# Turning TensorE's branch round so that the usual path follows in place

## The chip, the cores and the metric

The kernel runs on one core of one Trainium2 chip. The metric is the device time of one execution in microseconds, of several executions; "fast" runs are those that the record marks as such, as it does every run in this study (the granted clocks that it lists are 0.996 to 1.000). A ratio is the mean time of one kernel's fast runs over that of the other kernel's fast runs of the same rounds, so it is not quite the ratio of the medians that are quoted beside it. The interval behind a ratio is the 95% interval.

## The reference, cut to what matters

A transformer block with modulation: attention over a window of cached keys and values, then a feed-forward part with ReLU.

```python
mod = (silu(c) @ w_mod).reshape(1, 6, 1, -1)        # sa, ca, ga, sb, cb, gb
h = layernorm(x) * (1 + ca) + sa
x = x + ga * A(h, k_cache, v_cache, wq, wo)         # 32 query heads, 8 kv heads, window 512
h = layernorm(x) * (1 + cb) + sb
x = x + gb * (relu(h @ w1) @ w2)                    # 2048 rows, 512 -> 1792 -> 512
```

## The kernel before

The kernel has a fast path, which leaves the maximum out of the softmax, and a general path, which is right for any input. A flag computed on the chip tells whether the fast path's values were in range. Every engine loads the flag at a "cut" in its instruction stream, and branches. With these inputs the flag is 128 and the fast path's last part is all that is left to run.

```python
def engine(name, e):
    stream, n_ops = fast[name], cut[name]
    kb.emit(stream, e, 0, n_ops)                 # up to the cut
    e.wait_ge(sems[flag_ev[0]], flag_ev[1])
    v = e.value_load(flag[0:1, 0:1])             # L1829
    with e.If(v != 128):                         # L1830: not taken with these inputs
        kb.emit(stream, e, n_ops)
        ...                                      # all engines meet
        gkb.emit(general[name], e)               # the general path
    with e.Else():
        kb.emit(stream, e, n_ops)                # the usual path: a jump away
```

In the built program TensorE's stream has 3946 instructions up to the branch, 2997 in the first arm (last part and general path) and 225 in the second. TensorE's cut lies in the feed-forward part, in front of an output group:

```python
def y_group(b, tl, c0=0, c1=D, deng=None):       # 14 matmuls, then two VectorE operations
    for fc in range(FC):
        mm(bank[bk][:, c0:c1], h1T[...], w2_sb[:, fc, c0:c1], ...)
    kb.op(DVE, ... yt = bank * gbf ...)          # L1723, "evacuation"
    kb.op(DVE, ... yo = yt + x ...)              # L1725
    dma(ov[:, t, c0:c1], yo, ..., eng=deng)      # output, from SyncE's or ScalarE's queue

# the last group is split, so that the kernel's last matmuls are short
for a in ((0, D // 2, ACT), (D // 2, 3 * D // 4, SP), (3 * D // 4, D, ACT)): ...
```

At the end SyncE waits until the outputs have landed; then all engines meet (each with a DRAIN; TensorE's takes 1.2 us, from 555.55 to 556.74, and so ends 0.05 us after its last matmul, whose modelled end is at 556.69) and the program ends.

## Time and profile before

| | before |
|---|---|
| time, median | 560.52 us (3 runs, known when the prediction was made), 560.68 us (5 runs, those of the result) |
| span in the profile | 559.4 us |
| TensorE's branch, as recorded | 3.44 us |
| gap that it leaves between matmuls | 0.19 us |
| TensorE done / SyncE last at the end | 556.7 / 559.1 us |

TensorE's sequencer, which hands instructions to its array, is some way ahead of it: it loads the flag at 510.1 us, and the last matmul in front of the branch starts at 513.74, 3.6 us later. This lead is called run-ahead below.

### The profile page before, as it was taken

Reading aid. Unit: us, or ns where it says so; the run is one execution under the profiler, and the core shown is the slowest. Engines: PE = TensorE matmul, PEld = TensorE weight load, DVE = VectorE, ACT = ScalarE, POOL = GpSimd, SP = SyncE. Lnnn points to the kernel's source line nnn. Section 1 sums busy time; section 2 is a strip of 40 time slices with the busy share of each in tenths; the row PEclk is TensorE's granted clock in tenths of the full one; section 3 lists DMA queues with packets and bytes.
Section 4 is the critical chain, followed back from the end, with each engine's and each line's share of the span. In section 5 each row is a group of like instructions: output and inputs, shape, how many; then the busy total and the mean of one; then the engine's idle time right before and its main releaser. Section 6 shows DMA issues by size and latency. Waiting matters only on the chain.

```text
span 559.4 us, 9666 instructions
## 1 busy us (share of the span) xinstructions
PE 550.5 (98%) x4060; PEld 315.8 (56%) x4134; DVE 253.8 (45%) x551; ACT 348.9 (62%) x453; POOL 54.7 (10%) x53
## 2 busy tenths in 40 slices
PE   8999999999999999999999999999999999999998
PEld 4665555555555555555555555555555654444444
DVE  4455555553546544335445443333354448321134
ACT  4986666666666666666666666666666644432500
POOL 3000022004410000033000000332000000000000
DMA  9897763513114144352352412111215110210001
GB/s 268 248 207 174 143 169 46 114 39 76 40 38 76 39 73 117 58 133 57 94 95 57 76 40 39 39 39 38 39 39 76 39 30 0 44 34 23 22 29 47
DMA packets 113309, 42.67 MB, mean 76 GB/s; under 512 B 93928, under 2 KB 112104, under 8 KB 113256
## 3 DMA queue, kind: packets, MB, share of 16 engines
q1 hardware_dynamic: 112024, 40.82, 34.3%
q10 hardware_dynamic: 1232, 1.15, 0.6%
q8 instruction: 33, 0.54, 0.4%
q14 instruction: 20, 0.16, 0.1%
HBM read 18.35 MB, written 2.10 MB: 37 GB/s over the span
## 4 chain that ended last, share of the span: by engine, by line
PE 98%; issue 1%; DMA 1%; DVE 0%; SPq 0%; DVEq 0%
PE psS L1372 28%; PE psO L1372 27%; PE psQ L1372 23%; PE psW L1372 20%; DMA c_row<-in_c_dram 1%; DVE qT L1611 0%; DVE hT L1630 0%; SPq L1303 0%; DVE PT L1723 0%; DVE PT L1725 0%; PE psS L1375 0%; PE psO L1416 0%; DVE modc L1438 0%; DVEq L123 0%
## 5 line engine op out<-in xcount | busy, mean ns | idle before, releaser
L1493 ACT ACTIVATE PT<-psS 128x1024 bf16<-128x1024 f32 x256 | 262.7, 1028 | 128.2 <-PE psS L1372 128.1
L1372 PE MATMUL psS<-qT,kT 128*128 128x512 bf16 x508 | 150.9, 379 | 0.5 <-DVE qT L1611 0.4
L1372 PEld LDWEIGHTS psO<-v,PT 128*128 128x128 bf16 x2048 | 126.6, 98 | 30.2
L1372 PE MATMUL psO<-v,PT 128*128 128x129 bf16 x2048 | 137.0, 220 | 0.0
L1372 PE MATMUL psQ<-hT,wq 128*128 128x512 bf16 (+1 forms) x510 | 130.5, 377 | 0.3 <-DVE hT L1630 0.2
L1503 DVE RECIPROCAL rinv<-psO 128x4 f32<-128x4 f32 x128 | 23.3, 182 | 227.2 <-PE psO L1372 227.2
L1372 PE MATMUL psW<-wo,oT 128*128 128x512 bf16 x454 | 118.1, 379 | 3.0
L1504 DVE TENSOR_TENSOR o<-psO,rinv 128x512 bf16<-128x512 f32 x128 | 88.5, 691 | 4.9 <-DVE rinv L1503 0.5
L1372 PEld LDWEIGHTS psQ<-hT,wq 128*128 128x128 bf16 x512 | 49.9, 98 | 60.3 <-issue 0.6
L1372 PEld LDWEIGHTS psS<-qT,kT 128*128 128x128 bf16 x512 | 49.5, 98 | 58.9 <-ACT PT L1493 0.7
L1485 ACT ACTIVATE qT<-psQ 128x512 bf16<-128x512 f32 x126 | 74.7, 593 | 0.0
L1712 ACT ACTIVATE wq<-psS 128x512 bf16<-128x512 f32 x56 | 33.4, 597 | 49.3 <-PE psS L1372 48.9
L1372 PEld LDWEIGHTS psW<-wo,oT 128*128 128x128 bf16 x512 | 45.0, 98 | 32.9 <-DVE acc L1526 1.2
L1526 DVE TENSOR_TENSOR acc<-psW,acc 128x512 f32<-128x512 f32 x48 | 33.2, 691 | 6.5 <-PE psW L1372 6.5
L1372 PE MATMUL psO<-wmw,wq 128*128 128x512 bf16 (+1 forms) x165 | 32.8, 352 | 0.3
L1529 POOL TENSOR_TENSOR acc<-acc,gaf 128x512 f32<-128x512 f32 x12 | 15.6, 1303 | 146.7 <-DVE acc L1526 139.8
L1388 POOL TENSOR_TENSOR rstd<-rstd,cst 128x4 f32<-128x4 f32 x7 | 7.2, 1025 | 216.8 <-DVE rstd L1387 216.8
L1723 DVE TENSOR_TENSOR PT<-psO,gbf 128x512 f32<-128x512 f32 (+1 forms) x12 | 7.5, 624 | 40.4 <-PE psO L1372 40.4
L1372 PE MATMUL psS<-h2T,wmw 128*128 128x512 bf16 x109 | 25.0, 379 | 0.2
L1372 PEld LDWEIGHTS psO<-wmw,wq 128*128 128x128 bf16 x168 | 15.3, 98 | 16.5
L1372 PE MATMUL psS<-hT,wmw 128*128 128x512 bf16 x110 | 24.4, 379 | 0.1
L1382 DVE BATCH_NORM_STATS2 st<-x 128x6 f32<-128x512 bf16 x31 | 21.1, 681 | 4.8 <-DMA x<-in_A_x_dram 4.8
(85 smaller groups left out, 192.6 us busy)
## 6 DMA issues: line engine op xcount, KB each, us to landing
wo<-in_A_wo_dram SPq DMA_DIRECT2D x4, 1024.0 KB, 5.9
wq<-in_A_wq_dram SPq DMA_DIRECT2D x7, 512.0 KB, 4.6
wmw<-in_B_w_dram SPq DMA_DIRECT2D x14, 256.0 KB, 3.1
wmw<-in_w_mod_dram SPq DMA_DIRECT2D x5, 512.0 KB, 4.8
oT<-o SPq DMA_TRANSPOSE x128, 2.4
out_dram<-PT SPq DMA_DIRECT2D x15, 128.0 KB, 1.7
x<-in_A_x_dram SPq DMA_DIRECT2D x3, 512.0 KB, 4.3
v<-in_A_v_cache_dram SPq DMA_DIRECT2D x8, 128.0 KB, 3.8
```

Of the source, the lines that this page charges most:

```text
L1372: kb.op(PE, lambda e: e.matmul(out_ap, lhsT, rhs, start=start, stop=stop), reads=reads, group_writes=[R_b[k] for k in bk], signal=signal)
L1382: kb.op(DVE, lambda e: e.bn_stats(st[:, t, :], x_sb[:, t, :]), reads=[R_x[t]], writes=[R_st[t]])
L1388: kb.op(POOL, lambda e: e.tensor_tensor(rstd[:, sl], rstd[:, sl], cst[:, 0:1].to_broadcast([P, hi - lo]), op=ALU.pow), reads=R_rstd[sl] + ...
L1485: kb.op(ACT, lambda e: e.activation(qT[u % NQT][:, :], bank[bk], ACTF.Copy), reads=[R_b[bk]], writes=[R_qT[u % NQT]])
L1493: kb.op(ACT, lambda e: e.activation(PT[u % NPT][:, pr * 2:pr * 2 + 2, :], s_ps[pr][:, :, :], ACTF.Exp, scale=scale), reads=[R_b[pr * 2], R ...
L1503: kb.op(DVE, lambda e: e.reciprocal(rinv[:, u, :], o_ps[:, :, P]), reads=[R_b[5], R_b[6]], writes=[R_rinv])
L1504: kb.op(DVE, lambda e: e.tensor_tensor(o_sb[u % NOS][:, :, :], o_ps[:, :, 0:P], rinv[:, u, :].unsqueeze(2).to_broadcast([P, TPB, P]), op=A ...
L1526: kb.op(DVE, lambda e: e.tensor_tensor(acc[:, tl, :], bank[WBK], acc[:, tl, :], op=ALU.add), reads=[R_b[WBK], R_acc[tl]], writes=[R_acc[tl]])
L1529: kb.op(eng, lambda e: e.tensor_tensor(acc[:, tl, :], acc[:, tl, :], gaf[:, :], op=ALU.mult), reads=[R_acc[tl], R_ga], writes=[R_acc[tl]])
L1712: kb.op(ACT, lambda e: e.activation(h1T[b % 2][:, fc, :], bank[bk], ACTF.Relu), reads=[R_b[bk]], writes=[R_h1[b % 2][fc]], pre=all_events( ...
L1723: kb.op(DVE, lambda e: e.tensor_tensor(yt[i][:, c0:c1], bank[bk][:, c0:c1], gbf[:, c0:c1], op=ALU.mult), reads=[R_b[bk], R_gb], writes=[R_ ...
```

## The change

The intent is to take the jump of 3.44 us, and the fetch of its target (one packet on TensorE's instruction queue in 510.6 to 514.1 us), out of TensorE's usual path. The usual path follows the branch in place; the general path lies behind it and is jumped over at the end.

```diff
-                with e.If(v != 128):
+                def last_part():
+                    kb.emit(stream, e, n_ops)
+                def rerun():
                     kb.emit(stream, e, n_ops)
...
                     gkb.emit(general[name], e)
-                with e.Else():
-                    kb.emit(stream, e, n_ops)
+                if name == "pe":
+                    with e.If(v == 128):
+                        last_part()
+                    with e.Else():
+                        rerun()
+                else:
+                    with e.If(v != 128):
+                        rerun()
+                    with e.Else():
+                        last_part()
```

## The prediction

> **What bounds the kernel now.** I read the page first: busy times and the chain that ended last.

> ```profile
> PE 550.5 (98%) x4060; PEld 315.8 (56%) x4134; DVE 253.8 (45%) x551; ACT 348.9 (62%) x453; POOL 54.7 (10%) x53
> PE 98%; issue 1%; DMA 1%; DVE 0%; SPq 0%; DVEq 0%
> ```

> TensorE is the bound: its matmuls are 98% of the span and 98% of the chain. A change to TensorE's branch can matter only by gaps that the branch leaves between matmuls, or by what follows the last matmul. So next I read the source-line views of the flag's load, of the branch and of the block's end, which also list what is not counted as busy.

> The flag's load on TensorE (kind and count; least, median and largest ns; first and last start in us):

> ```profile
> L1829 PEldq TENSOR_LOAD <-flag x1: 493/493/493, 510.1 to 510.1; - x1
> ```

> The branch on the five engines:

> ```profile
> L1830 POOLq COMPARE_BRANCH  x1: 53/53/53, 478.9 to 478.9; - x1
> L1830 ACTq COMPARE_BRANCH  x1: 50/50/50, 508.9 to 508.9; - x1
> L1830 PEldq COMPARE_BRANCH  x1: 3440/3440/3440, 510.6 to 510.6; - x1
> L1830 DVEq COMPARE_BRANCH  x1: 72/72/72, 521.7 to 521.7; - x1
> L1830 SPq COMPARE_BRANCH  x1: 53/53/53, 522.8 to 522.8; - x1
> ```

> TensorE's branch is on record with 3440 ns, the others' with 50 to 72 ns. The reader should see the tempting number here: 3.44 us in a branch on the engine that is the bound. But what counts is when matmuls run. The timeline of 513.6 to 514.3 us:

> ```profile
> 513.31 0.81 PE L1372 MATMUL psO<-wmw,wq 128*128 128x512 bf16 x3
> 513.52 0.10 PEld L1372 LDWEIGHTS psO<-wmw,wq 128*128 128x128 bf16 x1
> 514.14 0.11 PEld L1372 LDWEIGHTS psQ<-wmw,wq 128*128 128x128 bf16 x2 [0.52 <-issue]
> 514.15 0.39 PE L1372 MATMUL psQ<-wmw,wq 128*128 128x512 bf16 x1
> ```

> Matmuls of 512 columns follow each other by 0.216 us here (14 of them make one output group in 3.02 us). Three from 513.31 would be followed by a fourth at 513.31 + 3 x 0.216 = 513.96; it came at 514.15, so the branch costs 0.19 us of TensorE time, not 3.44. VectorE's timeline confirms it: it takes each group's result when TensorE is done with it.

> ```profile
> 514.15 0.69 DVE L1723 TENSOR_TENSOR PT<-psO,gbf 128x512 f32<-128x512 f32 x1 [1.61 <-PE psO L1372]
> 517.38 0.69 DVE L1723 TENSOR_TENSOR PT<-psQ,gbf 128x512 f32<-128x512 f32 x1 [1.81 <-remote]
> 520.40 0.69 DVE L1723 TENSOR_TENSOR PT<-psO,gbf 128x512 f32<-128x512 f32 x1 [1.60 <-PE psO L1372]
> ```

> The first group behind the branch took 517.38 - 514.15 = 3.23 us, the next 520.40 - 517.38 = 3.02: a difference of 0.21. The reason is that TensorE's sequencer is ahead of its array: it loads the flag at 510.1, while the last matmul in front of the branch starts at 513.31 + 2 x 0.216 = 513.74. That is 3.6 us, or 17 matmuls with their 17 weight loads, already handed over. The load and the branch take 510.1 to 510.6 + 3.44 = 514.1, and only the last bit of it sticks out.

> The end of the program, from the source-line view of the block's end:

> ```profile
> L1844 POOLq DRAIN  x1: 129/129/129, 481.9 to 481.9; - x1
> L1844 PEldq DRAIN  x1: 1195/1195/1195, 555.5 to 555.5; - x1
> L1844 DVEq DRAIN  x1: 330/330/330, 557.1 to 557.1; - x1
> L1844 ACTq DRAIN  x1: 153/153/153, 557.8 to 557.8; - x1
> L1844 SPq DRAIN  x1: 13/13/13, 559.1 to 559.1; - x1
> ```

> All engines meet at the end. TensorE gets there at 555.5, waits 1.2 us for its own matmuls, and is done at 556.7; SyncE comes last at 559.1, since it waits for the last output transfer. So TensorE's sequencer has 559.1 - 555.5 = 3.6 us of slack there.

> [...] In the DMA view of 510.6 to 514.1 there is one packet on TensorE's instruction queue,

> ```profile
> q8 instruction: 1, 0.02, 1.8%
> ```

> and the page counts 33 packets and 0.54 MB on it, 16 KB each. GpSimd shows the same wait beside its short record: branch at 478.9, next instruction (its DRAIN) at 481.9, 3.0 us later with nothing else to do. [...] the trace has 50 to 72 ns for four engines[...]; the trace shows about 34 instructions of run-ahead (17 pairs), so I use 34.

> **The change part by part.**
> 1. Removed: the jump to the usual path in TensorE's stream. [...] Cost then: load 0.49 + some 0.06 between[...], against 3.6 us of run-ahead. All hidden. Gain: the 0.19 to 0.21 us gap, on the bound, and everything behind it moves forward by as much: -0.2 us.
> 2. Added: behind the usual path the general path now lies, so TensorE must jump over it to the block's end. That target is thousands of instructions away, so it is fetched: I take TensorE's own 3.44 us. It starts where the DRAIN starts now, since the sequencer has handed over the last matmul there: 555.5 - 0.2 = 555.3. It ends at about 558.8, and a DRAIN of an empty array follows (13 to 153 ns on the other engines): some 558.85 to 558.95.
> 3. What sets the end: SyncE's DRAIN, 559.1 - 0.2 = 558.9. So TensorE arrives within 0.1 us of SyncE. The run-ahead is smaller here (1.2 us against 3.6), because the last 28 matmuls are of 128 columns and take 1.58 / 28 = 0.056 us each; it is the wait for the output that hides the jump, not the array. If the fetch takes as long as at the branch, it just fits; if it is 0.3 us longer, those 0.3 us show. GpSimd's 3.0 would fit easily, but its packet is smaller (8 KB). I put the mean overrun at +0.1 us, with 0 to 0.6 as likely bounds.
> 4. Moved: nothing else. The other four engines keep their branch. ScalarE's sits in a 12.6 us wait for matmuls anyway. No matmul, tile or transfer changes.

> Sum: 560.5 - 0.2 + 0.1 = 560.4 us.

> **The rivals.**
> - *The branch's 3.44 us is real time on the bound*: then the change would give 557.1 us. Against it: matmuls run right through the branch, with one gap of 0.19 us. I give it almost nothing.
> - *The branch waits for the array to run empty, not for the fetch.* For it: the branch ends at 514.1, about when the last matmul's modelled end is (513.31 + 0.81 = 514.12), and TensorE alone has the long record. Then a branch not taken waits too, the gap stays, and the time is 560.5 to 560.6. Against it: the fetch is in the trace, and GpSimd, with nothing to drain, waits 3.0 us too. One in five.
> - *The jump at the end is not hidden.* If it can start only when the array is empty (556.5), or its fetch meets [...]the output transfers and takes 1 us more, TensorE comes to the end at about 559.9, up to 1 us behind SyncE: 561.2 to 561.4 us. One in six for more than half a microsecond.
> - *The fetch at the end is quick* (as on GpSimd): the whole 0.2 us is kept, 560.3 us.

> **Range and chances.** The mechanism moves the time between -0.25 and +0.9 us. The three runs of the kernel before lie between 560.33 and 560.81, so another median may be off by 0.3. The range of eight in ten is 559.8 to 561.2. 2% would be 11.2 us; neither the gain (at most the 3.44 of the record) nor the loss (one fetch) comes near. Chances: faster 0.005, same 0.99, slower 0.005.

> **What would show it right or wrong.** In the profile after: TensorE's branch on record with some 50 to 150 ns instead of 3440, and no 0.52 us weight-load gap behind it; the groups on either side of it 3.02 us apart at VectorE (step 1). A new jump of TensorE at about 555.3, 3 to 4 us long or followed by as long a silence, a fetch on its instruction queue in the last 4 us, where there is none now, and TensorE's DRAIN at about 558.8 instead of 555.5 (step 2). SyncE's DRAIN still last, or TensorE's by a few tenths (step 3). If the gap at the branch is still about 0.2 us, the second rival holds. If the last matmul ends 0.2 us earlier but the span is not shorter, the jump at the end has eaten the gain. A change of more than 1 us either way would mean that I missed a mechanism.

Passages that no trace or run of this case shows are cut out of the prediction, where it is marked. No term of its sum is among them: it came to 560.5 - 0.2 + 0.1 = 560.4 us, and does so still. Two terms are gone from what leads to it. In part 1 the cost that stays had a third term, the branch itself, which brought it to about 0.65 us. With the 50 to 72 ns of the other engines' branches it comes to 0.49 + 0.06 + 0.05 to 0.07 = 0.60 to 0.62 us, against the same 3.6 us of run-ahead. In the third rival one of the two things that the fetch might meet is gone. Its 1 us more, and the 150 ns as the upper end for the branch, are guesses, and no trace shows them.

## The result

| | before | after |
|---|---|---|
| median of 5 | 560.68 us (560.33 to 561.45) | 560.80 us (560.57 to 561.72) |
| ratio | | 1.0004 [0.9989, 1.0018] |
| span of the profiled run | 559.4 us | 558.8 us |

The time is the same. The profiled run of the changed kernel happened to be its fastest of five, so the two spans must not be subtracted; parts of the two traces have to be compared.

**At the branch** everything went as meant. The source-line view of TensorE's branches in the changed kernel (count; least, median and largest ns; first and last start):

```profile
L1846 PEldq COMPARE_BRANCH  x2: 90/1830/3570, 509.9 to 554.6; - x2
```

There are two now. The first is the branch at 509.9 us, 90 ns in place of 3440; it is over 0.64 us after the start of the flag's load (487 ns). The second, at 554.6 us, is the new jump over the general path: 3570 ns. The timeline across the branch (start, length, engine, count):

```profile
512.13 1.24 PE L1372 MATMUL psO<-wmw,wq 128*128 128x512 bf16 x5
...
512.99 0.53 PEld L1372 LDWEIGHTS psQ<-wmw,wq 128*128 128x128 bf16 x3
513.21 0.59 PE L1372 MATMUL psQ<-wmw,wq 128*128 128x512 bf16 x2
```

Five matmuls from 512.13 at 0.216 us each bring us to 513.21, where the next starts: no gap. Its weights are loaded at 512.99, ahead of it, and the 0.52 us wait for issue is gone. VectorE's evacuations (its first operation on each group's result) of the groups on either side:

```profile
513.41 0.69 DVE L1723 TENSOR_TENSOR PT<-psO,gbf 128x512 f32<-128x512 f32 x1 [1.61 <-PE psO L1372]
...
516.43 0.69 DVE L1723 TENSOR_TENSOR PT<-psQ,gbf 128x512 f32<-128x512 f32 x1 [1.61 <-PE psQ L1372]
```

They are 3.02 us apart, where they were 3.23 us apart before.

**At the end** the engines' DRAINs in the changed kernel:

```profile
L1857 DVEq DRAIN  x1: 332/332/332, 556.1 to 556.1; - x1
L1857 ACTq DRAIN  x1: 153/153/153, 557.2 to 557.2; - x1
L1857 PEldq DRAIN  x1: 68/68/68, 558.2 to 558.2; - x1
L1857 SPq DRAIN  x1: 13/13/13, 558.6 to 558.6; - x1
```

TensorE arrives at 558.2, with its jump over, and SyncE is still last, at 558.6. But SyncE has become later measured from VectorE's last operation, which begins at 557.05 before and at 556.11 after, and takes 0.29 us in both. From its end to the end of the span it is 559.36 - 557.34 = 2.02 us before, and 558.79 - 556.40 = 2.39 us after. The waits of SyncE in the last microseconds show where. Before:

```profile
SPq L1797 <- DMA out_dram<-PT: 1.2, 1, 1.2
SPq L123 <- DMA out_dram<-PT: 0.7, 1, 0.7
```

After:

```profile
SPq L123 <- DMA out_dram<-PT: 1.8, 1, 1.8
SPq L1797 <- DMA out_dram<-PT: 0.4, 1, 0.4
```

It now waits 1.8 us for an output that it waited 0.7 us for. That is no wait for TensorE; outputs land later. The last part of the output goes out in three transfers, the first and the third from ScalarE's queue and the second from SyncE's. The DMA view of the first one tells why. Before, in the half microsecond 556.9 to 557.4 (queue, packets, MB, share):

```profile
q10 hardware_dynamic: 144, 0.07, 45.5%
```

After, in 555.9 to 556.5:

```profile
q10 hardware_dynamic: 135, 0.06, 35.3%
```

And the rest of it, in 556.7 to 557.3:

```profile
q10 hardware_dynamic: 9, 0.00, 5.7%
```

The view counts 16 DMA engines; if a transfer's 144 packets are spread evenly over them, each has 9. In the changed kernel 135, 15 engines' worth, go through at once, and 9, one engine's worth, start 0.4 us after the rest are through. What lay in their way, as the author reads it, is the instruction packet that TensorE's jump fetched. In 554.6 to 558.7 of the changed kernel there is one on TensorE's instruction queue, and none before:

```profile
q8 instruction: 1, 0.02, 1.7%
```

The packet records have it from 555.67 to 556.79 us, 16,384 bytes. The nine late packets start at 556.78. The small output of SyncE's queue is split in the same way: 135 packets by 556.8, 9 packets from 557.23 on. The record does not name the DMA engine of a packet; that the nine share one with the fetch is inferred from the counts and the times. That a packet under way holds up the others on its engine is inference from this: the one packet of 16 KB took 1.1 us, where the median packet of 256 bytes takes 0.02.

The end is set by the third transfer, and in this trace that one is whole. It is late because its issue on ScalarE took longer. Before:

```profile
557.38 0.36 ACTq L1303 DMA_DIRECT2D out_dram<-PT  x1
```

After:

```profile
556.43 0.74 ACTq L1303 DMA_DIRECT2D out_dram<-PT  x1
```

The issue begins 0.03 us after VectorE's last operation in both, and is 0.38 us longer after the change, which is all that SyncE lost. It ends at 557.17, when the last of the first transfer's nine held packets are going through (557.24). That it waits for them fits the times, but no run shows it.

So there was a new theory: the gap of 0.2 us is gained, and the fetch of the jump at the end takes some 0.4 us from the outputs. The rivals were that the slower outputs are chance, that the turned branch as such does it, and, from the prediction, that branches wait for the array and not for the fetch.

### The profile page after: what moved, and what is told of

Its sections match the earlier page's. It is cut to its first block, busy times and chain, and to the rows that moved or that the text cites. A ratio compares the mean times of both kernels' runs of the same rounds, so it can differ in the third digit from the quotient of the medians.

```text
span 558.8 us, 9667 instructions
## 1 busy us (share of the span) xinstructions
PE 548.9 (98%) x4060; PEld 315.4 (56%) x4134; DVE 253.8 (45%) x551; ACT 348.9 (62%) x453; POOL 54.7 (10%) x53
## 4 chain that ended last, share of the span: by engine, by line
PE 97%; issue 1%; DVE 1%; DMA 1%
PE psS L1372 28%; PE psO L1372 27%; PE psQ L1372 23%; PE psW L1372 19%; DMA x<-in_A_x_dram 1%; DVE st L1382 0%; PE psS L1375 0%; DVE mv L1383 0%; DVE qT L1611 0%; DVE xn L1393 0%; DVE rstd L1588 0%; DVE PT L1723 0%; DVE PT L1725 0%; PE psW L1375 0%
## 5 line engine op out<-in xcount | busy, mean ns | idle before, releaser
L1372 PE MATMUL psS<-qT,kT 128*128 128x512 bf16 x508 | 150.9, 379 | 0.5 <-DVE qT L1611 0.4
L1372 PEld LDWEIGHTS psO<-v,PT 128*128 128x128 bf16 x2048 | 126.6, 98 | 30.2
L1372 PE MATMUL psO<-v,PT 128*128 128x129 bf16 x2048 | 137.0, 220 | 0.0
L1372 PE MATMUL psQ<-hT,wq 128*128 128x512 bf16 (+1 forms) x510 | 130.5, 377 | 0.2
L1372 PE MATMUL psW<-wo,oT 128*128 128x512 bf16 x454 | 118.1, 379 | 3.0
L1372 PEld LDWEIGHTS psQ<-hT,wq 128*128 128x128 bf16 x512 | 49.9, 98 | 60.2 <-issue 0.5
L1372 PEld LDWEIGHTS psS<-qT,kT 128*128 128x128 bf16 x512 | 49.6, 98 | 58.9 <-ACT PT L1493 0.7
L1372 PEld LDWEIGHTS psW<-wo,oT 128*128 128x128 bf16 x512 | 45.0, 98 | 32.9 <-DVE acc L1526 1.2
L1372 PE MATMUL psO<-wmw,wq 128*128 128x512 bf16 (+1 forms) x164 | 32.7, 352 | 0.3
L1723 DVE TENSOR_TENSOR PT<-psO,gbf 128x512 f32<-128x512 f32 (+1 forms) x12 | 7.5, 624 | 40.4 <-PE psO L1372 40.4
L1372 PE MATMUL psS<-h2T,wmw 128*128 128x512 bf16 x109 | 25.0, 379 | 0.2
L1372 PEld LDWEIGHTS psO<-wmw,wq 128*128 128x128 bf16 x168 | 15.4, 98 | 16.5
L1372 PE MATMUL psS<-hT,wmw 128*128 128x512 bf16 x110 | 24.4, 379 | 0.1
```

The lines of the kernel that those rows point to most:

```text
L1372: kb.op(PE, lambda e: e.matmul(out_ap, lhsT, rhs, start=start, stop=stop), reads=reads, group_writes=[R_b[k] for k in bk], signal=signal)
L1723: kb.op(DVE, lambda e: e.tensor_tensor(yt[i][:, c0:c1], bank[bk][:, c0:c1], gbf[:, c0:c1], op=ALU.mult), reads=[R_b[bk], R_gb], writes=[R_ ...
```

## The experiments

Twelve kernels ran, with runs of the kernel before between them. Kernels are compared only within the same rounds.

| kernel | median | before | ratio |
|---|---|---|---|
| after_again | 560.64 | 560.36 | 1.0008 [0.9995, 1.0022] |
| pe_plain | 561.46 | 560.36 | 1.0012 [0.9999, 1.0026] |
| late_before | 564.53 | 560.36 | 1.0072 [1.0058, 1.0087] |
| late_after | 560.91 | 560.36 | 1.0003 [0.9989, 1.0018] |
| pad_before | 560.46 | 560.38 | 0.9997 [0.9980, 1.0013] |
| pad_after | 562.21 | 560.38 | 1.0031 [1.0015, 1.0048] |
| all_turned | 561.52 | 560.38 | 1.0016 [0.9999, 1.0033] |
| actdve_turned | 561.53 | 560.38 | 1.0018 [1.0001, 1.0034] |
| near_after | 561.13 | 560.40 | 1.0011 [0.9997, 1.0024] |
| early_load | 560.11 | 560.40 | 0.9994 [0.9981, 1.0008] |
| before_again | 560.60 | 560.40 | 1.0007 [0.9994, 1.0021] |
| sp_far | 563.31 | 560.40 | 1.0050 [1.0035, 1.0066] |

Ratios within 0.1% of 1 say nothing here: the kernel before against itself (before_again) gives 1.0007. The traces resolve more. Each span is cut in three at VectorE's evacuations (L1723), as read from its timeline. The head ends at the first of them. The body goes to the last; in it lies TensorE's branch, and the view of waits lists none of TensorE's matmuls in it, before or after; the 0.19 us gap is read from the starts. The tail goes from the end of VectorE's last operation to the end of the span. (From the body's end to the tail's start it is 0.6 us in all of them.)

| trace | head, us | body, us | tail, us |
|---|---|---|---|
| before | 486.96 | 69.77 | 2.02 |
| before_again | 487.15 | 69.85 | 2.01 |
| pad_before | 486.71 | 69.73 | 2.01 |
| after | 486.21 | 69.57 | 2.39 |
| after_again | 486.21 | 69.57 | 2.50 |
| late_after | 487.21 | 69.57 | 2.59 |
| pe_plain | 487.93 | 69.57 | 2.00 |
| near_after | 486.67 | 69.57 | 2.01 |
| early_load | 486.19 | 69.57 | 2.01 |
| late_before | 486.87 | 73.24 | 2.02 |
| pad_after | 486.20 | 69.57 | 3.99 |
| all_turned | 486.32 | 69.57 | 3.63 |
| actdve_turned | 486.20 | 69.57 | 3.32 |
| sp_far | 486.30 | 70.05 | 4.71 |

The head varies by 1.7 us from run to run, in front of anything that the change touches; most of the noise of the timed runs lies there. Where nothing is lost, body and tail repeat closely: 69.57 us in nine bodies, 2.00 to 2.02 us in seven tails. With the taken branch at its old place the body varies with the branch's length (69.73 to 70.05 us), and the tail of the changed kernel varies too (2.39 to 2.59 us).

### The changed kernel again: after_again

No edit.

> The changed kernel once more, for a second profile and a tighter ratio. Theory (0.2 us gained at the branch, the end jump hidden): VectorE's evacuations of the last four batches again span 45.4 us from the first after the flag's branch on ScalarE to the last (45.6 before), TensorE's jump again 3.4 to 3.7 us, its DRAIN 0.1 to 0.4 us ahead of SyncE's; ratio 0.9990 to 1.0010. Rival (the jump's instruction fetch slows the last output's issue on ScalarE, which took 742 ns in the first profile against 363 before): again about 740 ns here, and a tail some 0.4 us longer than before. If 742 was chance: about 370 ns here and a tail of 2.4 us.

The body is 69.57 us, as in the first trace. TensorE's jump took 3.83 us, a little over what I had written, and its DRAIN was 0.2 us ahead of SyncE's. The last issue on ScalarE took 362 ns, not the 742 of the first trace: the rival as I put it, with a slow issue each time, fell. But the tail was long again, 2.50 us. Here the fetch lay 0.4 us later, from 556.11 to 557.07, and nine packets of each output were late all the same. This time the third transfer itself is split: 135 packets are through by 557.56, nine start at 557.70, and it lands 1.61 us after its issue where it took 1.13 us before. These 0.48 us are the whole growth of the tail. So the last output comes late in one of two ways: in its issue (0.38 us in the first trace and 0.57 us in late_after, where the issue took 932 ns, again the whole growth), or in its packets. Which of the two it is varies from trace to trace. What repeats is the held share of the outputs.

### TensorE without a branch: pe_plain

```diff
+                if name == "pe":
+                    kb.emit(stream, e)
+                    return
```

> TensorE without any branch: usual path straight through, no general path, no jump (right for these inputs alone). Theory: evacuations span 45.4 us as in the changed kernel, so all of the branch's cost is gone there too; TensorE reaches its DRAIN about 1.2 us before its array is done; time within 0.3 us of the changed kernel. Rival (the jump costs something at the end): 0.3 to 0.5 us faster than the changed kernel, with a last ScalarE issue of about 370 ns.

The body is that of the changed kernel, so turning the branch takes away all that the branch costs in the stream of matmuls. The tail is 2.00 us, 0.4 to 0.6 shorter than in three traces with the jump; here the rival's view of the end is borne out. The timed median, 561.46, is higher and not lower, a miss of the expected time. In the profiled run of this kernel it comes from the head, 487.93 us: its granted clock was 0.87 at 8 to 12 us and 0.70 at 12 to 16 us of the span, where the changed kernel's was 1.00, 500 us in front of the branch.

### The branch where the run-ahead is short: late_before and late_after

```diff
-                mlp.insert(len(mlp) - 2, lambda: cut_here("pe"))
...
+    mlp.insert(len(mlp) - 1, lambda: cut_here("pe"))    # in front of the last 128-column group
```

> The kernel before with TensorE's branch moved to just in front of its last group of 14 matmuls of 128 columns; taken jump as before. Theory (what is hidden is run-ahead): the sequencer is only 17 pairs ahead, 14 of 0.056 us and 3 of 0.109, about 1.1 us; load and branch take some 4.05 us, so about 2.9 us come out as a gap in front of the last group, and the 0.2 us gap at the old place is gone: +2.7 us against the kernel before. Rival (a branch waits for the array to run empty and the fetch is nothing): gap about 0.2 us, time unchanged.

> The changed kernel with TensorE's branch moved to the same late place. Theory: load and a branch not taken take about 0.65 us, under the 1.1 us of run-ahead: no gap; the jump at the end is as in the changed kernel. Time as the changed kernel's, within 0.3 us, so 2.7 us faster than late_before. Rival (a branch waits for the array to run empty): a gap of 0.2 us or more at the new place.

In late_before TensorE's timeline has the gap:

```profile
554.67 0.94 PE L1372 MATMUL psO<-wmw,wq 128*128 128x128 bf16 x14
558.39 1.68 PE L1372 MATMUL psO<-wmw,wq 128*128 128x128 bf16 x14 [2.78 <-issue]
```

The second group begins 558.39 - 554.67 = 3.72 us after the first. A group takes 14 x 0.056 = 0.78 us, so 2.94 us are lost, as expected. But the body grew by 73.24 - 69.57 = 3.67 us. The other 0.7 us are in the group itself, 1.68 us against 0.94, and the view by windows has the cause in its granted clock (window, length, busy time of TensorE, weight load, VectorE, ScalarE and GpSimd, clock, DMA share, GB/s):

```profile
554.00:555.40 1.40, 1.40 (x22) 1.32 (x20) 1.22 (x4) 0.00 (x0) 0.00 (x0) 1.00 0.00 0
...
558.30:560.20 1.90, 1.68 (x14) 1.41 (x14) 0.09 (x1) 0.00 (x0) 0.00 (x0) 0.50 0.04 9
```

Behind this gap of just under 3 us the granted clock was 0.50, where it had been 1.00 in front of it. The time, +4.0 us by the ratio, missed the expected +2.7 by that and by the head's noise.

In late_after there is no gap: the body is 69.57 us, and the kernel is 3.6 us faster than late_before. In these traces a taken branch cost what was longer than the run-ahead: 0.19 us of 3.44 at the old place, 2.94 us of 3.53 here. The one that fell through, 90 ns, cost nothing even at the end of the program. And the rival that a branch waits for the array falls: the one not taken took 90 ns and was over at 555.27, while the last matmul in front of it began at 555.74 only.

### Idle matmuls behind the last group: pad_before and pad_after

```diff
+    for i in range(38):
+        mm(bank[WBK][:, 0:P], ones[:, :], ones[:, :], True, True, [R_ones], [WBK], i == 37)
```

> The kernel before with 38 idle matmuls of 128 columns behind TensorE's last group (2.1 us of array time that nothing waits for). Theory: TensorE comes to the end at about 558.8 us of the span instead of 556.7, still 0.3 us ahead of SyncE: time within 0.3 us of before.

> The changed kernel with the same 38 matmuls. Theory (the jump at the end fills the slack that the output transfer gives): the jump starts 2.1 us later, ends at about 560.9 us of the span, and TensorE's DRAIN becomes the last; +1.5 to +2.0 us against the kernel before. Rival (the jump is cheap and only its record is long): no change, as for pad_before.

In pad_before the 2.1 us (38 x 0.056) cost nothing: the ratio is 0.9997 and the tail 2.01 us. In pad_after the last DRAINs are:

```profile
L1859 SPq DRAIN  x1: 13/13/13, 558.2 to 558.2; - x1
L1859 PEldq DRAIN  x1: 68/68/68, 560.1 to 560.1; - x1
```

TensorE is last, 1.9 us behind SyncE: the jump is real time that had filled the slack at the end. By the ratio the time is +1.7 us, as expected. There is a second reading in the same trace. The fetch comes 2 us later here, at 557.70, behind the outputs. SyncE's wait for L123 is back at 0.7 us and its DRAIN comes 1.8 us after VectorE's last operation, as before. The fetch doesn't meet the outputs here, and none is held: each transfer has its 144 packets together, and the last lands 1.5 us after the start of its issue, as before.

### The jump without the fetch: near_after

```diff
                 def rerun():
+                    if name == "pe":
+                        e.wait_ge(meet, len(fast))
+                        return
```

> The changed kernel with TensorE's general path cut to one instruction (right for these inputs alone), so that its jump at the end has its target one step on[...]. New theory (the jump's instruction fetch holds back the output transfers on one of the 16 DMA engines): no fetch in the last 4 us, a jump record under 0.3 us, the last transfer whole, and a tail from VectorE's last operation to the end of 2.01 us, where the changed kernel had 2.40, 2.50 and 2.59 in three traces; the gap at the branch stays away (evacuations span 45.4 us). Rival (turning the branch as such, or chance, makes the tail longer): a tail of 2.4 us or more here too.

```profile
L1849 PEldq COMPARE_BRANCH  x2: 85/132/180, 510.4 to 555.0; - x2
```

With its target one step on, the jump took 180 ns, there is no instruction packet on TensorE's queue in the last 4 us, and the tail is 2.01 us. The turned branch is kept and the fetch is gone, and with it the held outputs. TensorE also comes to the end some 3 us sooner here, so this run alone doesn't part the fetch from TensorE's coming late; pad_after does, where TensorE is later than in any other trace but the fetch comes behind the outputs, and SyncE isn't delayed. So it is the fetch, not the turned branch and not chance.

The packet records of all 14 traces say the same. In seven an instruction packet lies across the last outputs (after, after_again, late_after, late_before, all_turned, actdve_turned, sp_far), and in each of them at least one of the last transfers is split into 135 and 9 packets. In the other seven no instruction packet does, and all are whole.

### The flag loaded earlier: early_load

```diff
+                n_load = n_ops - 28 if name == "pe" else n_ops
-                kb.emit(stream, e, 0, n_ops)
+                kb.emit(stream, e, 0, n_load)
                 e.wait_ge(sems[flag_ev[0]], flag_ev[1])
                 v = e.value_load(flag[0:1, 0:1])
+                kb.emit(stream, e, n_load, n_ops)
```

This is the branch of the kernel before, a taken jump, with the load of the flag moved 28 matmuls ahead.

> The kernel before, with TensorE's load of the flag put two output groups (28 pairs) ahead of its branch; the branch itself as before. Theory: the load's 0.55 us no longer stands between the last handed-over matmul and the branch, so 3.44 us of branch lie against 3.6 to 3.8 us of run-ahead: the gap of 0.2 us is gone (evacuations span 45.4 us, 3.02 us apart across the branch), and there is no jump at the end, so the tail is 2.01 us. It should be 0.2 us under the kernel before and 0.4 to 0.6 under the changed one; the timed ratio to before 0.9985 to 1.0010, too small a step to show.

The branch took 3573 ns and left no gap: VectorE's evacuations across it are at 513.38 and 516.40.

```profile
513.38 0.69 DVE L1723 TENSOR_TENSOR PT<-psO,gbf 128x512 f32<-128x512 f32 x1 [1.60 <-PE psO L1372]
...
516.40 0.69 DVE L1723 TENSOR_TENSOR PT<-psQ,gbf 128x512 f32<-128x512 f32 x1 [1.60 <-remote]
```

Body 69.57 us and tail 2.01 us: it has the gain of the changed kernel and not its cost. Its five runs, 560.02 to 560.28, lie lowest of all, though by the ratio's interval it isn't told apart from the kernel before. By body and tail it is 0.2 us better than the kernel before and 0.4 to 0.6 us better than the changed one.

### The kernel before again: before_again

No edit.

> The kernel before against itself, to see what the timed ratio does when nothing differs: ratio 0.999 to 1.001. Profile: gap of 0.2 us at the branch (evacuations 3.2 us apart across it), tail 2.01 us.

Tail 2.01 us; the gap is 0.28 us, with a branch of 3.52 us. The ratio of 1.0007 is the measure of what a timed ratio can show here.

Four traces with the taken branch at the old place give a small law. The branch took 3.40, 3.44, 3.52 and 3.72 us (pad_before, before, before_again, sp_far), and the body was 0.16, 0.20, 0.28 and 0.48 us over 69.57: the gap is the branch's length less 3.24 us in all four. So 3.24 us of it were hidden behind the queued matmuls.

### The other engines: actdve_turned, all_turned and sp_far

```diff
-                if name == "pe":
+                if name in ("pe", "act", "dve"):     # actdve_turned
+                if True:                             # all_turned
+                if name == "sp":                     # sp_far, and 800 sem_inc at the general path's end
```

> TensorE, ScalarE and VectorE turned, SyncE and GpSimd as before. Theory: ScalarE's jump begins after its last output issue (about 557.7 us of the span) and takes 3.0 us, so it ends at 560.7 against SyncE's 559.1: about +1.5 us against before (1.0 to 2.0). VectorE's begins at 557.1 to 557.3 and would end 0.4 us sooner.

> All five engines turned as TensorE was. Theory: SyncE's jump begins only after its wait for the last output, at about 559.0 us of the span, and no work lies beside it; with GpSimd's 3.0 us for such a fetch, +2.8 us or more against before (2.5 to 3.5). Rival (jumps are hidden anyway): no change.

In actdve_turned ScalarE's jump began at 556.80 and its DRAIN came at 559.40, 2.6 us later, 0.6 us behind SyncE's: the time is +1.0 us by the ratio, the low end of what was expected. In all_turned I expected +2.8 us or more and got +0.9. The DRAINs there:

```profile
L1857 SPq DRAIN  x1: 52/52/52, 559.5 to 559.5; - x1
L1857 ACTq DRAIN  x1: 81/81/81, 559.8 to 559.8; - x1
```

SyncE's jump began at 559.0, and its DRAIN followed at 559.5, with no packet between on the instruction queue that those engines use (the one packet in 558.5 to 559.6 is on TensorE's): nothing was fetched for it then. SyncE's whole program is short (some 455 instructions when built). Whether that is why, sp_far tests.

> SyncE alone turned, with 800 more instructions (never run) at the end of its general path, so that its jump's target is out of reach. In the kernel with all five turned, SyncE's next instruction came 0.47 us after its jump began, and no instruction packet lay between. Theory (a jump is cheap where the target has been fetched; SyncE's whole program was short enough): now 2.6 to 3.2 us as on ScalarE and VectorE there, all of it behind the last output: +2.5 to +3.0 us against before. Rival (SyncE's jumps are always cheap): +0.3 us.

```profile
L1849 SPq COMPARE_BRANCH  x2: 38/46/53, 522.4 to 558.9; - x2
...
L1860 SPq DRAIN  x1: 53/53/53, 561.4 to 561.4; - x1
```

With 800 more instructions between, 2.5 us pass from the jump at 558.9 to the DRAIN at 561.4, and the time is +2.8 us by the ratio. The record of the jump itself says 38 ns; the wait lies behind it, unrecorded, and that it is for a fetch is inference. The jump is not all of it: 0.36 us is a held output again. An 8 KB packet on the other engines' instruction queue, from 557.63 to 558.21 and so before SyncE's jump, lay across the third transfer; nine of its packets started at 558.21, and it landed 1.50 us after its issue where it took 1.13 us before. The rival, that SyncE's jumps are cheap, falls: 800 more instructions in front of the target made 2.5 us of 0.47.

## Why the prediction was right or wrong

The predicted time was 560.4 us with a range of 559.8 to 561.2; it measured 560.8, with 0.4 us of that within what a repeat does. That it lies in the range says little, since the kernel before, at 560.7, does too. Taken step by step:

- *What bounds the kernel, and the 0.19 us gap.* Right. The body lost 0.20 us (69.77 to 69.57), and the same 69.57 came out without any branch.
- *Step 1, a branch not taken is hidden.* Right: 90 ns, no gap, even where the run-ahead was only about 1 us (late_after).
- *Step 2, a jump at the end of 3.44 us, starting where the DRAIN had started.* Right: 3.57 us in the first trace, 3.83 and 3.75 in two others.
- *Step 3, what sets the end.* This step failed in its mechanism, and its term was mis-sized. It put +0.1 us on TensorE's coming late to the end, and took SyncE's arrival as untouched. SyncE stayed last in all three traces, but later by itself: the tail grew from 2.01 to 2.39, 2.50 and 2.59 us, a mean of +0.48 us, where a fetched packet lay across the outputs and nine of 144 packets came late (near_after, without the fetch, has 2.01). That it held one DMA engine's share, and with it the landing of the last output, is inference. The third rival had fetch and outputs meet, but with the fetch as the one that pays. Had SyncE not been delayed, it would have come 1.8 us after VectorE's last operation, at 558.2 in the first trace, and TensorE, done at 558.3, would have been last by 0.1 us; worked out in the same way from the other two traces it is 0.4 us (after_again) and 0.3 us (late_after). So the arrival was sized within its bounds of 0 to 0.6 us; the larger effect covers it.
- *The sum.* With the measured terms it is -0.20 + 0.48 = +0.3 us in place of -0.1. The two timed ratios, 1.0004 and 1.0008, amount to +0.2 and +0.4 us, which fits, but a kernel against itself gave +0.4; so the sign of the change in time rests on the traces and not on the clock.
- *The rivals.* That 3.44 us are real time on the bound was wrong at this place, and nearly right at another (late_before: 2.94 us). That a branch waits for the array was wrong. That the fetch at the end is quick was wrong as well: the jump took 3.57 us.

What stays open: which DMA engine carried which packet isn't in the records; why ScalarE's last issue was long in the first trace and in late_after, and not in after_again, isn't known; and what makes the head vary by 1.7 us is known for one trace alone (a lower clock in its first 16 us) and not for those that had the full clock and still differ by 1.0 us.

## What to carry to other kernels

A branch with 3.44 us on record cost 0.19 us here, what was longer than the sequencer's run-ahead, so read the gap between matmuls and not the record; where it does show, loading the flag earlier can hide it without any new jump, as it hid one of 3.57 us here (early_load). In this kernel, turning the branch moved the jump to a far target, 3.57 us on record, to the end of the path and didn't remove it. Ask there both whether that engine has slack and what the fetched packet will meet on the DMA engines, since an output that everything waits for can be what pays: here the tail grew by 0.4 to 0.6 us.
